# Head-wise loads of eight tokens per partition, turned by column tiles, in an attention + MLP kernel

## The chip, the cores and the metric

The kernel runs on one core of one Trainium2 chip. The metric is the device time of one execution in microseconds (us). Executions of one kernel agree within about 0.3%, and all timed comparisons below use runs of the fast state; two kernels had a single look, whose state is unknown, and of them only durations of single instructions are read. "Start" below means the first matmul that multiplies by `w_in`, "end" the end of the last matmul, both read from the trace of the profiled run; "dense part" is the time between, "tail" the time from the end to the end of the span. Each set of rounds ran on one chip, with the kernel before run along (medians of 206.90 to 207.19 us).

One thing bears on every reading of the first 14 us: TensorE's clock. The records of the granted clock begin only when it first rises to full; the profile prints 1.00 ahead of that, but there the clock is half. In the kernel before, plain matmuls of 128 columns start 107 ns apart until 9.3 us and 56 ns apart from 10.4 us on, and the first record is at 10.33.

## The reference, cut to what matters

```python
# q, k, v: (4, 8, 768, 64) fp32, drawn * 0.1; w_in (512, 2048), w_out (2048, 512); n_global 8, n_local 96
scores = q @ k.T / 8 + bias(-slope[h] * distance)      # masked to a local window of 96 and 8 global keys
a = softmax(scores)
x = (a @ v)  -> (3072, 512)
h = x @ w_in
out = (h - tanh(h)) @ w_out
```

Because q and k are drawn with a factor of 0.1, the distance bias dominates the scores. The comparison with the reference therefore hardly notices q and k in a wrong order.

## The kernel before

The work is cut into 24 tiles of 128 queries with all 8 heads. A tile is loaded (q, k, v), its q and k are turned so that the head dimension lies on partitions, scores are multiplied, exponentiated and masked, multiplied with v, scaled, and turned again to become the moving operand of the first product (`w_in`). Pairs of tiles then take the second product (`w_out`), for some groups as a Strassen product of seven. The program does not state an order: a planner in it simulates all engines with assumed durations and writes each engine's instructions in the order that comes out. Each engine then works through its own instructions in that order.

The loads: 256-byte rows, one token of one head each, that is 8 rows per partition. The three first (k of tile 0, q of tiles 0 and 1) are hardware loads in fp32 that VectorE casts to bf16; all others are issued by GpSimd and are cast on the way.

```python
hw_loads = {("k", 0): SP, ("q", 0): SP, ("q", 1): ACT}
...
def rows(src, u):
    b, i = tiles[u]
    return src[b, :, i * P : (i + 1) * P, :].rearrange("h p d -> p h d")
```

The turn: four plain transposes of 128 columns into one PSUM bank, in bf16, then one copy out.

```python
def pe_T(bank, src):
    t = bank.bitcast(BF16)
    for p in range(NP):                                  # NP = 4 pairs of heads
        nc.tensor.transpose(t[:, p * P : (p + 1) * P], src[:, p * P : (p + 1) * P], ident)
...
pl.op(("T", nm, u), PE, 0.24, lambda ...: pe_T(...))
pl.op(("Te", nm, u), [(DVE, 0.345), (ACT, 0.48)], None, lambda ...: copy(...))
```

Masking and the product with v work on all eight heads at once; the second product is in Strassen form for the groups in FAST; the last group's last two products share one bank:

```python
FAST = set(range(5, 14))
...
pl.op(("M", u, o), DVE, 0.61, lambda ...: a_M(u, o), after=[E half 0, E half 1, mask half 0, mask half 1])
...
HOME = {3: ("in", 0), 4: ("in", 1), 1: ("one", 0), 5: ("mid", 0), 2: ("mid", 1), 7: ("out", 0), 6: ("out", 1)}
...
if g == LAST:
    for t, kk in enumerate((7, 6)):
        pl.op(("cs", g, t), DVE, 0.335, ...)             # sum of the bank and what was kept
        pl.op(("st", us[t], 1), SP, 0.6, ...)            # store of 128 KB
```

The softmax here doesn't subtract the row's maximum and nothing guards it: scores larger than these inputs give would overflow.

## Time and profile before

| | before |
|---|---|
| time, median of 3 runs | 207.09 us (206.95 to 207.3) |
| span of the profiled run | 205.1 us |
| start / end / tail | 16.16 / 201.38 / 3.76 us |
| first tile's q landed, its first scores | 6.83, 9.61 us |
| first two parts of `w_in` landed | 14.8, 18.2 us |

The prediction shows the lines. In a row of the timeline the columns are start, length, engine, line of the program, operation, written tile, read tiles, shapes and count, and in brackets how long the engine had been idle and what ended that. Landing times are of the DMA records in the trace. One line is added here because the change replaces it: the turn of k tiles before, as durations of the single matmuls (least, median and most in ns). Matmuls overlap, so the pace is seen from start to start: it is 56 ns at the full clock.

```profile
L461 PE MATMUL bank<-ident,kb x28: 219/219/314, 6.5 to 41.0; 128*128 128x128 bf16 x28
```

### The profile page before, as it was taken

The numbers are of one execution on the slowest core, as the hardware profiler recorded it, in microseconds if no ns is written. First come the engines' busy times: TensorE is split into PE (matmuls) and PEld (weight loads), VectorE is DVE, ScalarE is ACT, GpSimd is POOL, SyncE is SP. The second block draws the span as 40 slices with busy tenths as digits, with TensorE's granted clock in tenths as the row PEclk, the third lists the DMA queues.
The fourth block names the chain that finished last, engine by engine and source line by source line (L and its number), as shares of the span: only waits on it lengthen the run. The fifth ranks groups of instructions, "written<-read, shape, count | busy, mean of one in ns | idle before, by whom it ended". The sixth has DMA issues, their size and how long they took to land.

```text
span 205.1 us, 5929 instructions
## 1 busy us (share of the span) xinstructions
PE 197.7 (96%) x2339; PEld 167.3 (82%) x2339; DVE 176.4 (86%) x387; ACT 139.7 (68%) x326; POOL 68.1 (33%) x83
## 2 busy tenths in 40 slices
PE   7789999999999999999999999999999999999992
PEld 5568997579867779889898898898898898888881
DVE  5698899989886888899999879979979979699683
ACT  6699878275787886996987777667677665434310
POOL 8985363680552250542251351351350000000000
PEclk9999999999999999999999999999999999999999
DMA  6999999999999999999999999998998504002023
GB/s 141 158 184 199 186 204 192 170 186 151 178 196 203 135 101 162 82 139 194 124 89 226 106 101 109 189 114 111 184 116 90 151 6 128 3 0 102 3 102 102
DMA packets 110971, 27.28 MB, mean 133 GB/s; under 512 B 103008, under 2 KB 108128, under 8 KB 110944
## 3 DMA queue, kind: packets, MB, share of 16 engines
q0 software_dynamic: 76512, 13.24, 88.5%
q1 hardware_dynamic: 32864, 13.38, 34.2%
q10 hardware_dynamic: 1568, 0.30, 0.8%
q8 instruction: 18, 0.29, 0.6%
q14 instruction: 9, 0.07, 0.1%
HBM read 27.30 MB, written 6.29 MB: 164 GB/s over the span
## 4 chain that ended last, share of the span: by engine, by line
PE 88%; DMA 7%; DVE 2%; ACT 1%; issue 0%; DVEq 0%
PE bank L476 39%; PE bank L347 28%; PE bank L517 7%; PE bank L412 5%; DMA qT<-qb 5%; PE bank L431 3%; PE bank L433 2%; DMA ot<-in_q_dram 2%; PE bank L461 2%; PE bank L714 1%; DVE pd L422 1%; ACT x L448 0%; DVE kT L402 0%; DVE qb L402 0%; ACT pd L417 0%
## 5 line engine op out<-in xcount | busy, mean ns | idle before, releaser
L476 PE MATMUL bank<-xT,w_in_bf 128*128 128x256 bf16 (+1 forms) x896 | 95.2, 257 | 0.2 <-ACT pd L417 0.2
L476 PEld LDWEIGHTS <-w_in_bf 128*128 128x128 bf16 x896 | 75.6, 98 | 8.7 <-issue 0.3
L803 ACT ACTIVATE th<-bank 128x512 f32<-128x512 f32 x96 | 56.8, 610 | 32.0 <-PE bank L476 28.8
L485 DVE TENSOR_TENSOR g<-bank,th 128x512 bf16<-128x512 f32 x80 | 53.0, 683 | 8.2 <-ACT th L803 7.9
L626 POOL DMA_DIRECT2D kb<-in_k_dram x23 | 20.3, 884 | 72.9 <-PE bank L476 68.6
L347 PEld LDWEIGHTS <-hb 128*128 128x128 bf16 x416 | 40.1, 98 | 5.2
L347 PE MATMUL bank<-bsum,hb 128*128 128x256 bf16 x256 | 32.9, 273 | 0.0
L417 ACT ACTIVATE pd<-bank 128x512 bf16<-128x512 f32 x48 | 26.1, 601 | 6.4 <-PE bank L412 6.4
L321 DVE TENSOR_TENSOR hb<-g 128x1024 bf16<-128x1024 bf16 x45 | 29.6, 683 | 0.2
L417 ACT ACTIVATE po<-bank 128x512 bf16<-128x512 f32 x40 | 22.3, 623 | 0.0
L626 POOL DMA_DIRECT2D vb<-in_v_dram x24 | 21.6, 899 | 1.8 <-DMA w_out_bf<-in_moe_w_out_dram 1.6
L448 ACT ACTIVATE x<-bank,rden 128x64 bf16<-128x64 f32 x84 | 19.4, 316 | 3.6 <-DVE rden L440 3.2
L422 DVE TENSOR_TENSOR pd<-pd,mk 128x1024 bf16<-128x1024 bf16 x24 | 16.5, 688 | 5.6 <-ACT pd L417 5.5
L626 POOL DMA_DIRECT2D qb<-in_q_dram x22 | 19.9, 904 | 3.7 <-DMA w_out_bf<-in_moe_w_out_dram 3.5
L347 PE MATMUL bank<-w_out_bf,hb 128*128 128x256 bf16 x160 | 20.6, 273 | 0.0
L347 PE MATMUL bank<-bsum,g 128*128 128x256 bf16 x144 | 18.4, 273 | 0.0
L321 DVE TENSOR_TENSOR ot<-bank,sum 128x512 f32<-128x512 f32 (+1 forms) x21 | 13.8, 661 | 2.2 <-PE bank L347 1.8
L347 PEld LDWEIGHTS <-g 128*128 128x128 bf16 x144 | 13.8, 98 | 1.8
L412 PE MATMUL bank<-qT,kT 64*128 64x128 bf16 x352 | 14.5, 219 | 0.4 <-DMA qT<-qb 0.2
L422 DVE TENSOR_TENSOR po<-po,mk 128x1024 bf16<-128x1024 bf16 x20 | 13.7, 685 | 1.2 <-ACT po L417 1.1
L412 PEld LDWEIGHTS <-kT 64*128 64x128 bf16 x352 | 10.3, 95 | 5.1 <-issue 4.3
L431 PE MATMUL bank<-vb,pd 128*128 128x65 bf16 x192 | 14.1, 193 | 0.1
(57 smaller groups left out, 184.2 us busy)
## 6 DMA issues: line engine op xcount, KB each, us to landing
out_dram<-ot SPq DMA_DIRECT2D x9, 512.0 KB, 3.4
vb<-in_v_dram POOLq DMA_DIRECT2D x24, 128.0 KB, 5.7
kb<-in_k_dram POOLq DMA_DIRECT2D x23, 128.0 KB, 5.0
qb<-in_q_dram POOLq DMA_DIRECT2D x22, 128.0 KB, 5.4
w_out_bf<-in_moe_w_out_dram POOLq DMA_DIRECT2D x4, 512.0 KB, 13.3
w_in_bf<-in_moe_w_in_dram POOLq DMA_DIRECT2D x3, 512.0 KB, 10.8
out_dram<-ot SPq DMA_DIRECT2D x5, 256.0 KB, 4.5
w_in_bf<-in_moe_w_in_dram POOLq DMA_DIRECT2D x2, 256.0 KB, 8.9
```

Of the source, the lines that this page charges most:

```text
L321: eng_of(e).tensor_tensor(out=out, in0=x, in1=y, op=ALU.add if sign > 0 else ALU.subtract)
L347: nc.tensor.matmul(o, a, b, start=(f == 0), stop=(f == CH - 1))
L412: nc.tensor.matmul(t[hh][:, p * P : (p + 1) * P], kt[r, p, :], qt[r, p, :], start=True, stop=True)
L417: nc.scalar.activation(dst, t, AF.Exp, bias=0.0, scale=scale)
L422: nc.vector.tensor_tensor(out=p, in0=p, in1=mk[:, m, :, :], op=ALU.mult)
L431: nc.tensor.matmul(o, pd[:, slot(h), :], vd[:, h, 0 : Dh + 1], start=True, stop=w is None)
L448: nc.scalar.activation(x[:, h, :], t[:, h, 0:Dh], AF.Copy, bias=0.0, scale=rd[:, h, :])
L476: nc.tensor.matmul(t[:, (f - fa) * n : (f - fa + 1) * n], w_in_bf[j][:, c, fo : fo + P], xt[:, c, 0:n], start=(c == 0), stop=(c == CD - 1),)
L485: nc.vector.tensor_tensor(out=dst, in0=t.rearrange("q (b n) -> q b n", n=n), in1=th.rearrange("q (b n) -> q b n", n=n), op=ALU.subtract,)
L517: nc.tensor.matmul(o, gblk(g, f, f + 1, t * P, t * P + P)[:, 0, :], w_out_blk(f, 0, DM), start=(f == 0), stop=(f == CF - 1),)
L626: pl.op(key, POOL, 0.88, lambda e, u=u, src=src, dst=dst: nc.gpsimd.dma_start(out=dst(), in_=rows(src, u)), after=[prev and ("issue", prev ...
L803: pl.op(("th", g, f), ACT, 0.48, lambda e, g=g, f=f: nc.scalar.activation(buf("th", ("th", g, f)), buf("bank", ("h", g, f)), AF.Tanh, bias ...
```

## The change

Its intent: q and k of the first four tiles are loaded with 2 KB rows. A partition then holds 8 tokens of one head (16 partitions for each of 8 heads) instead of one token of all heads, so the usual transpose does not fit. Eight pairs of matmuls do the turn instead: for token j of the eight, the stationary operand is the 64 columns of that token, the moving operand a slice of the identity that picks the even or the odd heads, and the two heads of a pair are written to the two halves of the partitions by two column tiles of TensorE. Around it: masks, products with v and scaling by head parity for the first six tiles; group 4 in Strassen form; three banks and three stores at the last group; a new order of tiles and of loads.

```diff
-    TILES = [(1, 0), (0, 0), (0, 1), (1, 1), (0, 2), (3, 0), (0, 3), (3, 1), (2, 0), (2, 1), ...]
+    TILES = [(1, 0), (0, 0), (0, 1), (1, 1), (0, 2), (3, 0), (3, 1), (3, 2), (1, 2), (2, 0), ...]
-    FAST = set(range(5, 14))
-    NPE = 7
-    NPX = 8
+    FAST = set(range(4, 14))
+    N8 = 4
+    HSPLIT = 6
+    NPE = 8
+    NPX = 6
...
+    TJ = 8
+    def rows8(src, u):
+        b, i = tiles[u]
+        return src[b, :, i * P : (i + 1) * P, :].rearrange("h (t j) d -> t h (j d)", j=TJ)
...
+    def pe_T8(bank, src):
+        o = bank.rearrange("e (p t j) -> e p t j", p=NP, j=TJ)
+        i8 = ident.rearrange("k (t p s) -> k s p t", p=NP, s=2)
+        for j in range(TJ):
+            for s in range(2):
+                nc.tensor.matmul(
+                    o[s * Dh : (s + 1) * Dh, :, :, j], src[:, j * Dh : (j + 1) * Dh], i8[:, s], start=True, stop=True,
+                )
...
-                pl.op(("T", nm, u), PE, 0.24,
-                      lambda e, u=u, nm=nm: pe_T(buf("bank", ("T", nm, u)), buf(nm + "b", (nm + "b", u))),
+                pl.op(("T", nm, u), PE, 0.55 if u < N8 else 0.24,
+                      lambda e, u=u, nm=nm: (pe_T8 if u < N8 else pe_T)(buf("bank", ("T", nm, u)), buf(nm + "b", (nm + "b", u))),
...
+            if u < HSPLIT:
+                for hh in range(2):
+                    pl.op(("M", u, o) if hh else ("Mp", u, o), DVE, 0.335, lambda e, u=u, o=o, hh=hh: a_M(u, o, hh, hh + 1),
+                          after=[("E", u, o, hh), masks[hh], ("issue", ("Mp", u, o)) if hh else None])
...
-            for t, kk in enumerate((7, 6)):
+            for t, c0, c1, key, tag in ((0, 0, DH, ("P", g, 7), "out2"), (1, 0, DH // 2, ("Pp", g, 6), "out"),
+                                        (1, DH // 2, DH, ("P", g, 6), "out3")):
```

## The prediction

> **What bounds the kernel now.** I read, in this order: the busy shares and the slices of the page, the chain of waits that ended last, the timeline of the first 25 us, the table of stretches over the same part, and the timeline of the last 10 us.
>
> From the page:
>
> ```profile
> PE 197.7 (96%) x2339; PEld 167.3 (82%) x2339; DVE 176.4 (86%) x387; ACT 139.7 (68%) x326; POOL 68.1 (33%) x83
> PE   7789999999999999999999999999999999999992
> DMA  6999999999999999999999999998998504002023
> PE 88%; DMA 7%; DVE 2%; ACT 1%; issue 0%; DVEq 0%
> ```
>
> TensorE is on the chain for 88% of the span, and only the first three slices and the last are not full. (A busy TensorE can still be slow, so I count paces below.) The DMA engines are full from the second slice to beyond the middle. The candidates for a gain are therefore the first 16 us, TensorE's amount of work, and the last 4 us.
>
> The chain in order of time gives the paces of undisturbed stretches:
>
> ```profile
> 0.74 4.60 DMA ot<-in_q_dram
> 14.09 0.96 ACT x L448 x4
> 16.16 1.05 PE bank L476 x16
> 17.70 1.79 PE bank L476 x32
> 36.70 3.45 PE bank L517 x16
> 40.16 0.87 PE bank L347 x8
> 193.52 7.87 PE bank L347 x72
> ```
>
> The first product runs at 56 ns for each 128-column matmul (1.79/32), the direct second product at 216 ns for 512 columns (3.45/16), a Strassen product at 109 ns for 256 columns (0.87/8). Priced so, the work after 16.16 us is: first product 640 x 0.109 + 256 x 0.056 = 84.2; Strassen 560 x 0.109 = 61.2; direct 64 x 0.216 = 13.8; scores, some 290 at 35 ns, 10.2; probabilities times v, 330 at 30 ns, 10.1; transposes 48 x 0.056 = 2.7. Sum 182.2 us, while 16.16 to the last matmul's end at 201.4 is 185.2. The missing 3 us is about what some 36 changes between the score form and the full form cost at 0.1 us (a block of eight after one takes 0.98 instead of 0.87). So from 16.16 us there is practically no stall. The start of the dense part sets the end.
>
> The timeline before it:
>
> ```profile
> 6.51 0.61 PE L461 MATMUL bank<-ident,kb 128*128 128x128 bf16 x4 [1.43 <-DVE kb L402]
> 7.50 0.57 DVE L402 CAST qb<-ot 128x512 bf16<-128x512 f32 x1
> 9.61 0.61 PE L412 MATMUL bank<-qT,kT 64*128 64x128 bf16 x8
> 10.25 1.09 ACT L417 ACTIVATE pd<-bank 128x512 bf16<-128x512 f32 x2 [2.02 <-PE bank L412]
> 11.77 0.68 DVE L422 TENSOR_TENSOR pd<-pd,mk 128x1024 bf16<-128x1024 bf16 x1
> 15.11 0.88 POOL L626 DMA_DIRECT2D kb<-in_k_dram  x1 [0.89 <-DMA w_in_bf<-in_moe_w_in_dram]
> 15.59 0.42 DVE L402 COPY xT<-bank 128x512 bf16<-128x512 bf16 x1
> 18.51 0.74 POOL L598 DMA_DIRECT2D w_out_bf<-in_moe_w_out_dram  x1 [1.77 <-DMA w_in_bf<-in_moe_w_in_dram]
> ```
>
> Two strands meet at 16.16: the first tile's attention (its q, cast at 7.50, to its transposed output, done at 16.01), and the first part of w_in. GpSimd's waits say when weights landed: its 16th issue is released by w_in at about 15.1, the 18th at 18.4. I take these for the first and second part of w_in (the 8th and 10th issues); the second is about when the rest of the first tile's product can begin. The strand of loads has no more than 1 us of slack.
>
> **What the Trainium skill says.** "DMA: Bandwidth & Descriptors", section "Why small descriptors are slow (HBM only)", puts about three cycles of overhead on a packet: 11 instead of 8 cycles for 256 bytes. The trace agrees in size. GB/s in the next rows counts bytes as landed, in bf16, half of what these loads read:
>
> ```profile
> 8.00:10.00 2.00, 2.00 (x22) 1.64 (x20) 1.20 (x4) 0.23 (x2) 2.00 (x3) 1.00 2.42 154
> 12.00:14.00 2.00, 1.84 (x37) 1.41 (x32) 2.00 (x7) 2.00 (x5) 2.00 (x3) 1.00 1.25 205
> ```
>
> With 256-byte rows in flight it is 154 GB/s, so 128 KB take 0.85 us; with 2 KB rows of the weights 205 GB/s, so 0.64 us. "TensorEngine Tiling (Array Packing)", sections "Key Properties" and "Restrictions": tiles can run in parallel, a change of tiling drains the engine, and column tiling excludes fast weight load. The trace shows the drain (the 0.98 above); this kernel has no column tile, so the rest is not shown. "PSUM — Partial Sum Buffer", section "PSUM bank collisions raise a hardware error", says two engines must not touch a bank at once; that is why, in the tail, both last additions wait for the very last matmul.
>
> **The change part by part.**
>
> (1) Loads. All eight q and k loads of the first four tiles come before the first part of w_in, before and after, so each saves 0.85 - 0.64 = 0.21 us of a full DMA: 8 x 0.21 = 1.7 us. Three are hardware loads in fp32, for which I have no clean rate, so I take 1.5 us. The first w_in part then lands at about 13.6 and the second at 16.9. The first tile's hardware loads, which took 3.9 and 5.6 us to land, should take 3 to 4: its q is castable at about 5 to 5.5 instead of 7.
>
> (2) Turning. A tile was turned by four matmuls (4 x 0.056 = 0.22 us); now by 16 with 64 columns each. With 30 ns, the pace of the 65-column matmuls here, they take 0.5 us, with the lost fast weight load up to 0.9. Eight turns cost 2 to 5 us more, in a stretch where TensorE multiplies zeros or waits: of 16.16 us only about 4.8 are useful. Little of it should reach the end. The PSUM copy out is now fp32: about 0.6 instead of 0.42 us, 8 x 0.2 = 1.6 us of VectorE and ScalarE, of which 0.4 lies on the first tile's strand.
>
> (3) Halves by head parity for six tiles. For the first tile, mask (0.68 in one piece), product, reciprocal and scaling can start with the first exponential; I count 0.5 us off the strand from 9.61 to 16.01. With (1) it is ready near 13.6 to 14.2. The strand gains 1.8 to 2.4, the loads 1.5 at the second weights part. I take the dense start 1.9 us earlier, all told.
>
> (4) Group 4 goes to Strassen: 32 x 0.216 = 6.9 against 56 x 0.109 = 6.1 us: 0.8 us less. It costs VectorE about 5.5 us (five sums of 0.68, evictions) in a region where it has 10 to 25% free, and ScalarE is relieved by 1.2.
>
> (5) Transposes elsewhere: one more tile's q and k on TensorE, two tiles' outputs fewer: eight matmuls each way, zero.
>
> (6) The tail. Now:
>
> ```profile
> 199.47 1.91 PE L347 MATMUL bank<-bsum,hb 128*128 128x256 bf16 x16
> 201.42 0.76 DVE L321 TENSOR_TENSOR ot<-bank,sum 128x256 f32<-128x256 f32 x2 [0.33 <-PE bank L347]
> 201.87 0.82 SPq L547 DMA_DIRECT2D out_dram<-ot  x2
> ```
>
> Both additions (0.76) follow the last matmul and two issues (0.82) follow the first. With three banks, only one addition of 128 columns (estimate 0.3, from 0.42 for 256) and one issue of 0.41 remain behind it: the last issue ends near 202.2 instead of 202.7. Gain 0.5 us.
>
> (7) New order of tiles and of issues, one more buffer each for kb, qb and x: with no stall to remove, zero, give or take 0.5.
>
> Sum: 1.9 + 0.8 + 0.5 = 3.2 us. I give back 0.2 for turns that fall into the dense part and their extra drains. 207.1 - 3.0 = 204.1; the tuning hints that the start was fitted to the new loads, so I round to **204.0 us**.
>
> **Rivals.** (a) Vector and Scalar bind the head: VectorE is busy all of 12 to 16 us and ScalarE all of 12 to 16, and each first-phase tile needs from VectorE more (four subtractions, two masks, scaling, copies: about 6 us) than TensorE's 3.6 us of first product. Then the earlier loads buy under 1 us: 205.5. For it: these rows; against it: ScalarE idles 2 us ahead of 10.25 and VectorE several short times before it. (b) The turn is slow: at 0.9 us or more, eight turns (7 us) plus 3 us of other useful work overfill the 9 us before the start; the head gains nothing: 205.8. For it: no fast weight load; against it: the pairs may overlap. (c) Loads alone bind the start: the attention is ready first, and TensorE fills the time to the second w_in part with the first quarter of four tiles (4 x 0.89 us): 2.8 us in the head, 203.1 or less. For it: the 1 us between 15.1 and 16.16; against it: (a). (d) Strassen's sums at group 4 make VectorE the bound from 40 to 70 us, eating the 0.8: 204.8.
>
> **Range and chances.** (a), (b) and (d) pull up by 0.8 to 1.8, (c) down by 1; they exclude each other in part. Range 202.5 to 205.7. Faster by over 2% means under 202.95, which asks for (c) and a little more: 0.23. Slower by 2% (211.2) would need a new stall that lasts through the dense part: 0.01. Within 2%: 0.76.
>
> **What would show it.** The first w_in matmul at 13.5 to 14.8 us instead of 16.16; GpSimd's waits for w_in ending 1.5 us earlier; the fp32 loads landing within 4 us; a turn's 16 matmuls within 0.5 to 0.6 us; 616 + 8 Strassen and 32 direct matmuls; no TensorE idle between the start and the last 4 us; last matmul to end of the span 3.2 instead of 3.7 us. I am wrong if the dense start moves by less than 1 or more than 2.8 us, if TensorE has gaps between 16 and 70 us, or if a turn takes near 1 us.

## The result, and the profile after

The changed kernel took **209.44 us** in the median (209.32 to 209.52, 4 runs), the kernel before 207.19 us in the same rounds (206.95 to 207.44, 4 runs). A ratio here and below is the mean time of one kernel's runs over the mean of the other's of the same rounds, so it is not quite the ratio of the medians: 1.0108, 95% interval 1.0091 to 1.0126. Executions over 1.5% slower than the fastest of the same kernel are left out of the means. By the measure of 2% that is "same", but it is 1% slower, on the wrong side of zero and well outside the range of 202.5 to 205.7.

| | before | after | difference | predicted |
|---|---|---|---|---|
| start | 16.16 | 18.54 | +2.38 | -1.9 |
| dense part | 185.22 | 184.67 | -0.55 | -0.6 (Strassen -0.8, +0.2 back) |
| tail | 3.76 | 4.47 | +0.71 | -0.5 |
| span | 205.14 | 207.68 | +2.54 | -3.0 |

So the middle did what was predicted and both ends went the other way. The page of the kernel after, against the lines of before in the prediction:

```profile
PE 200.5 (97%) x2464; PEld 173.0 (83%) x2464; DVE 183.4 (88%) x403; ACT 140.7 (68%) x332; POOL 66.3 (32%) x83
PE   6899999999999999999999999999999999999991
PE 89%; DVE 5%; DMA 2%; issue 1%; ACT 0%; DVEq 0%; ACTq 0%
```

TensorE is busier than before, 200.5 instead of 197.7 us, which is no gain: it is busy with the turns. The third digit of its row, which was 8 before, is now full. The chain of waits in order of time (start, length, what) shows where:

```profile
5.96 5.02 PE bank L477 x80
10.98 0.55 PE bank L425 x16
11.53 1.05 PE bank L477 x16
...
14.09 1.03 PE bank L477 x16
...
15.47 1.03 PE bank L477 x16
...
18.61 1.00 PE bank L499 x16
```

L477 is the new turn. It is on the chain eight times: five turns back to back take 5.02 us, the three others 1.03 to 1.05 us each, 8.1 us in all. The timeline over the same stretch tells how the first tile gets behind:

```profile
10.91 0.62 PE L425 MATMUL bank<-qT,kT 64*128 64x128 bf16 x16
11.34 2.06 ACT L430 ACTIVATE pd<-bank 128x512 bf16<-128x512 f32 x4 [3.99 <-PE bank L425]
12.60 0.69 DVE L415 CAST qT<-bank 128x512 bf16<-128x512 f32 x1 [0.89 <-PE bank L477]
13.21 0.75 DVE L435 TENSOR_TENSOR pd<-pd,mk 128x512 bf16<-128x512 bf16 x2
14.02 1.10 PE L477 MATMUL bank<-ident,kb 128*64 128x64 bf16 x16
15.40 1.10 PE L477 MATMUL bank<-ident,kb 128*64 128x64 bf16 x16
16.41 0.88 POOL L656 DMA_DIRECT2D qb<-in_q_dram  x1 [2.64 <-DVE x L464]
18.54 1.07 PE L499 MATMUL bank<-xT,w_in_bf 128*128 128x128 bf16 x16
```

The first scores start at 10.91 instead of 9.61, since five turns stand ahead of them in TensorE's order. The first mask starts at 13.21 instead of 11.77: VectorE takes its work in order too, and ahead of the mask stands the copy out of a later turn, for which it waited 0.89 us while the first exponentials were done. From mask to start it is 5.33 us instead of 4.39, with two more turns in between. So 1.44 us of the delay of 2.38 arose before the mask and 0.94 after it. GpSimd, which also waits in order, was held for 2.64 us at 16.41 by this strand; with two more loads standing ahead of it in the new order, the first part of `w_out` was issued at 19.1 instead of 16.0 and landed at 31.2 instead of 29.3.

How long a turn is inside: 1.10 us less the 0.30 us that a single one of these matmuls lasts, over the seven steps from pair to pair, is 0.115 us per pair. In the records the two matmuls of a pair start 2 to 8 ns apart. They do run side by side; it is the pair that is slow, 115 ns for 64 columns where 65 columns of another product take 30 ns. The clock is not the reason: the turns ahead of 10.2 us, where it rose to full, have the pace of those behind it.

The tail of the kernel after, timeline of the last 5 us:

```profile
203.35 0.82 DVE L324 TENSOR_TENSOR ot<-bank,sum 128x256 f32<-128x256 f32 x3 [0.46 <-PE bank L354]
203.80 1.59 SPq L570 DMA_DIRECT2D out_dram<-ot  x3
```

One store issue more stands in line (1.59 us for three instead of 0.82 for two); 0.30 us of that is the second of the three, which took 0.68 us. And the first of the three sums, whose product was done 0.88 us before the end of TensorE, does not start until 0.14 us after that end.

### The profile page after: what moved, and what is told of

Same layout as the page of the kernel before. It is cut to its first block, busy times and chain, and to the rows that moved or that the text cites. A ratio compares the mean times of both kernels' runs of the same rounds, so it can differ in the third digit from the quotient of the medians.

```text
span 207.7 us, 6184 instructions
## 1 busy us (share of the span) xinstructions
PE 200.5 (97%) x2464; PEld 173.0 (83%) x2464; DVE 183.4 (88%) x403; ACT 140.7 (68%) x332; POOL 66.3 (32%) x83
## 4 chain that ended last, share of the span: by engine, by line
PE 89%; DVE 5%; DMA 2%; issue 1%; ACT 0%; DVEq 0%; ACTq 0%
PE bank L499 41%; PE bank L354 28%; PE bank L425 5%; PE bank L477 4%; PE bank L540 3%; PE bank L445 3%; PE bank L447 2%; DMA ot<-in_k_dram 2%; PE bank L484 2%; DVE ot L324 1%; DVE hb L324 1%; DVE pd L435 1%; DVE g L508 1%; DVE po L435 1%; DVE qT L415 0%
## 5 line engine op out<-in xcount | busy, mean ns | idle before, releaser
L354 PEld LDWEIGHTS <-hb 128*128 128x128 bf16 x464 | 44.1, 98 | 5.7
L656 POOL DMA_DIRECT2D kb<-in_k_dram x20 | 17.7, 884 | 74.0 <-PE bank L499 63.4
L354 PE MATMUL bank<-bsum,hb 128*128 128x256 bf16 (+1 forms) x288 | 35.4, 270 | 0.0
L324 DVE TENSOR_TENSOR hb<-g 128x1024 bf16<-128x1024 bf16 x50 | 32.6, 684 | 0.2
L656 POOL DMA_DIRECT2D qb<-in_q_dram x20 | 17.8, 888 | 9.3 <-PE bank L499 5.5
L354 PE MATMUL bank<-bsum,g 128*128 128x256 bf16 x160 | 20.4, 273 | 0.0
L435 DVE TENSOR_TENSOR pd<-pd,mk 128x1024 bf16<-128x1024 bf16 (+1 forms) x30 | 17.1, 578 | 3.1 <-ACT pd L430 3.1
L324 DVE TENSOR_TENSOR ot<-bank,sum 128x512 f32<-128x512 f32 (+2 forms) x24 | 15.2, 641 | 3.6 <-PE bank L354 3.5
L354 PEld LDWEIGHTS <-g 128*128 128x128 bf16 x160 | 15.5, 98 | 2.0
L435 DVE TENSOR_TENSOR po<-po,mk 128x1024 bf16<-128x1024 bf16 (+1 forms) x23 | 14.1, 618 | 1.5 <-ACT po L430 1.3
L413 ACT COPY vb<-vb 8x512 bf16<-8x512 bf16 x14 | 8.6, 614 | 9.9 <-PE bank L447 9.9
## 6 DMA issues: line engine op xcount, KB each, us to landing
w_out_bf<-in_moe_w_out_dram POOLq DMA_DIRECT2D x4, 512.0 KB, 10.3
```

The source lines that it names most:

```text
L324: eng_of(e).tensor_tensor(out=out, in0=x, in1=y, op=ALU.add if sign > 0 else ALU.subtract)
L354: nc.tensor.matmul(o, a, b[:, c0:c1], start=(f == 0), stop=(f == CH - 1))
L413: nc.scalar.copy(out=dst, in_=src)
L435: nc.vector.tensor_tensor(out=p, in0=p, in1=mk[:, m, s0 * NP : s1 * NP, :], op=ALU.mult)
L656: else nc.gpsimd.dma_start(out=dst(), in_=rows(src, u)),
```

## The experiments

Where an expectation speaks of T, that is the theory that the turn is slow and lies on the way to the start; the rivals are named in the texts: the loads, the tail, the order of the plan. Every kernel is a change of the kernel after, unless the text says that it is of the kernel before. In e1, e2, h1, v5 and the f kernels the durations that the planner assumes are those of the kernel after (h1 and v5 add one small copy to the plan); in the others it plans anew, and the order can shift with the edit.

### Is it the turn? A plain one in its place

```diff
-        (pe_T8: 16 matmuls)
+        for p in range(NP):
+            nc.tensor.matmul(bank[:, p * P : (p + 1) * P], src[:, p * P : (p + 1) * P], ident, start=True, stop=True)
```

This is the kernel after with four plain matmuls of 128 columns; q and k of four tiles are wrong.

> The changed kernel with its 16 small matmuls of a turn replaced by four ordinary ones of 128 columns (a wrong result on purpose; same loads, same order of instructions, same fp32 copy out). Theory T (the turn holds TensorE in front of the first tile: 8 x 1.03 us instead of 8 x 0.22, so some 6 us of it on the way): the first w_in matmul comes at 15 us or earlier instead of 18.5, the time falls from 209.4 to 206.4 or less. Rival L (loads no sooner, DMA engines out of step): start at 17.5 or later, 208.5 or more. Rival O (the new order of tiles and issues makes the head late): the same as L.

Measured: 207.82 us, ratio to before 1.0048 (1.0033 to 1.0063); start 16.84, dense part 184.63, tail 4.57. The start comes 1.7 us earlier than after's and the time falls by 1.6, so most of the loss at the head is the turn. Two of its turns, one at the half and one at the full clock, and the start:

```profile
10.98 0.61 PE L474 MATMUL bank<-ident,qb 128*128 128x128 bf16 x4
12.95 0.39 PE L474 MATMUL bank<-ident,kb 128*128 128x128 bf16 x4
16.84 1.07 PE L494 MATMUL bank<-xT,w_in_bf 128*128 128x128 bf16 x16
```

But the start is still later than before's 16.16, though this kernel has the larger rows and the halves by parity: with a turn as cheap as the old one, the head has gained nothing. The first tile's q landed at 7.54 us, and the clock was half until 12.4 us. The result lies between what the turn as the only cause asked for (206.4 or less) and what the rivals did (208.5 or more): the turn is the larger part and not the whole.

### Why does a pair take 115 ns?

The candidates are the loading of 64-column weights, the moving operand, whose columns are 16 bytes apart (every eighth element of the identity), and the writes, 32 bytes apart in PSUM. Three kernels, all wrong, take them one at a time:

```diff
 f2: stationary operand of 128 columns, so no column tile; moving operand and writes strided as before
+            c = min(j, TJ - 2) * Dh
+            nc.tensor.matmul(o[:, :, :, j], src[:, c : c + 2 * Dh], i8[:, s], start=True, stop=True)
 f4: as f2, but the moving operand contiguous
+            nc.tensor.matmul(o[:, :, :, j], src[:, c : c + 2 * Dh], ident[:, 0:Dh], start=True, stop=True)
 f5: as f2, but the writes contiguous
+            nc.tensor.matmul(bank[:, j * Dh : (j + 1) * Dh], src[:, c : c + 2 * Dh], i8[:, s], start=True, stop=True)
```

> The changed kernel with the same 16 matmuls of 64 moving columns in a turn, but with 128 columns stationary instead of 64 (full array, a wrong result on purpose). If the 64 ns of each are the slow loading of a 64-column weight tile, the pace falls to about 30 ns, a turn to 0.5 us, and the time to about 207.5. If it is the number of matmuls or the 32-byte strides of their writes: 64 ns and 209.3 as before.

> One look. As the wide turn (16 matmuls, 128 columns stationary, 64 moving, wrong result on purpose), but the moving operand is contiguous and only the writes to PSUM keep their 32-byte stride. The pair of small matmuls took 117 ns in the changed kernel, a wide one 115 ns. If the strided writes cost it: still about 115 ns a matmul, a turn of 1.9 us. If the strided reads of the moving operand cost it: about 30 ns, a turn of 0.5 to 0.6 us.

> One look. The counterpart: contiguous writes, moving operand with its 16-byte stride, 128 columns stationary (wrong result on purpose). If the strided reads cost it: about 115 ns a matmul; if the writes: about 30 ns. If both this and the run with strided writes are near 30 ns or both near 115, neither stride alone is the cause and slow weight loading is left.

One turn of sixteen in the chain of waits of each, first f2, then f4, then f5:

```profile
19.41 1.85 PE bank L478 x16
```

```profile
13.84 0.89 PE bank L478 x16
```

```profile
20.51 1.83 PE bank L478 x16
```

f2: 116 ns per matmul, now one after another, so the kernel got slower still: 216.32 us, ratio 1.0459, start 25.33. Weights of 128 columns do not help; the loading of 64-column weights was not the limit. f5, with the writes put right, keeps 114 ns. f4, with the moving operand put right, needs 56 ns (208.81 and 219.68 us for f4 and f5, single looks of unknown state, so only the durations count). The clocks differ, half for all of f5's turns and full for all of f4's, but f2 settles it: its pace is 116 ns both ahead of 9.5 us, where its clock rose, and behind. At the full clock, then, it is 116 ns with both strides (f2) and 56 ns with the strided writes alone (f4). The moving operand's step of 16 bytes is the cost, and the strided write is a smaller one, about twice the 30 ns of a contiguous product. This says also that a pair of column tiles costs as much as one such matmul: the tiling worked.

The Trainium skill has this, in a place where I did not look: "SBUF — State Buffer", section "Door 1: The DMA port swizzle", notes that SBUF is read in lines of 16 bytes, that full bandwidth needs at least two accesses to a line, and that PSUM has lines of 8 bytes, so that non-contiguous access slows matmuls. The steps here, 16 and 32 bytes, reach a new line with every element. The trace agrees, with 114 and 56 ns against some 30.

### A turn that is right and contiguous

The moving operand is a permuted copy of the identity, made once; the writes are contiguous; the copy out of PSUM does the permutation.

```diff
+    ident8 = cpool.tile([P, 2, Dh], BF16, name="ident8")   # even and odd heads, packed
 ...
-                    o[s * Dh : (s + 1) * Dh, :, :, j], src[:, j * Dh : (j + 1) * Dh], i8[:, s], start=True, stop=True,
+                    bank[s * Dh : (s + 1) * Dh, j * Dh : (j + 1) * Dh], src[:, j * Dh : (j + 1) * Dh], ident8[:, s, :],
+                    start=True, stop=True,
 ...
-     copy(e, dst, bank)
+     copy(e, dst.rearrange("d p (t j) -> d p t j", j=TJ), bank.rearrange("d (j p t) -> d p t j", j=TJ, p=NP))
```

> The changed kernel, right result, with the same 16 column-tile matmuls of a turn, but contiguous on both sides: a permuted identity stored contiguously as moving operand, contiguous writes, and the order put right by the copy out of PSUM. If strides cost the 117 ns of a pair: 30 to 60 ns a pair, a turn of 0.3 to 0.6 us, start near 16.5, 206.9 to 207.5. If it is the loading of 64-column weights[...]: still about 109 ns, a turn of 0.9 to 1.0 us, 209.

Two turns in the timeline of h1:

```profile
10.84 0.64 PE L476 MATMUL bank<-ident,qb 128*64 128x64 bf16 x16
...
14.37 0.44 PE L476 MATMUL bank<-ident,kb 128*64 128x64 bf16 x16
```

and one stretch of its table of stretches, in which the number after the busy times is the granted TensorE clock:

```profile
10.00:12.00 2.00, 2.00 (x33) 1.40 (x30) 1.33 (x3) 1.68 (x4) 2.00 (x4) 0.50 1.23 204
```

At the full clock a turn takes 0.44 us from first start to last end: 0.244 without the last matmul's own 0.196, or 35 ns per pair. At the half clock, granted from 7.2 to 14.0 us in this run, it is 0.64 us. TensorE had been busy for only 0.30 of the 2 us from 4 to 6 and 0.78 of the next 2. The Trainium skill, "TensorE: Matmul & The Clock Gate", section "What's actually happening", gives half the clock as the state at first and again after an idle window of some 3.4 us. The trace agrees with the half, 0.50, but the stretch before the fall was not idle: from 3.8 to 7.2 us TensorE was busy for 1.2 us.

The time is 207.28 us (207.11 to 207.4), ratio 1.002 (1.0005 to 1.0035), 2.16 us less than after. By the traces, 1.35 of the 2.35 us in the span are the start (17.19), 0.34 the dense part (184.33), and 0.66 the tail (3.81), to which the turn contributes nothing; more on that below. The start is still 1 us later than before's. All four runs of h1 show the low mean clock of 0.982 to 0.983, so the long half clock belongs to this kernel's time; what it may be worth is told with v5 below.

A middle way was to give a partition 4 tokens of a pair of heads, 1 KB rows, with 8 matmuls of 128 moving columns (right):

```diff
-        return src[b, :, i * P : (i + 1) * P, :].rearrange("h (t j) d -> t h (j d)", j=TJ)
+        return src[b, :, i * P : (i + 1) * P, :].rearrange("(p s) (t j) d -> t p s (j d)", s=2, j=TJ)   # TJ = 4
 ...
+                nc.tensor.matmul(o[s * Dh : (s + 1) * Dh, :, :, j], src[:, c : c + Dh], ident, start=True, stop=True)
```

> The changed kernel with 4 tokens of a head pair per partition (1 KB rows) and a turn of 8 matmuls (64 columns stationary, 128 moving) instead of 16 of 64 by 64; right result. If the 64 ns of a small matmul are the loading of its 64 weight columns, a turn takes 8 x 64 = 0.5 us and the time falls by about 2 us to 207.4 (theory T). If the pace grows to 128 ns (moving columns or the strided writes set it), a turn stays at 1.0 us and the time at 209.4. Rivals L and O: 209.4 whatever the turn takes.

Measured: 206.87 us, ratio 0.9997 (0.9982 to 1.0012), start 16.04, dense part 184.69. Pairs follow each other by 109 ns, but there are four of them instead of eight. It is level with before.

### Are the loads worth anything?

e3 is the kernel after with the old rows and the old turn everywhere (`N8 = 0`).

> The changed kernel with the loads and turns of the kernel before (256-byte rows, four transposes), all else kept. T: the head is as before or better (start 15.5 to 16.5), the dense part 0.6 us shorter, the tail 0.8 longer: 206.5 to 207.5. L: the same. O: start still near 18 us, 208.5 to 209.5.

Measured: 206.78 us, ratio 0.9994 (0.9978 to 1.0011); start 16.52, dense part 184.83, tail 3.82. Without the new rows and the new turn most of what they cost at the head is gone (16.52 against 18.54, before 16.16); what is left of the change is level with before.

The three first loads are hardware loads. v5 is h1 with the old rows and the old turn for these three alone:

```diff
-    ... if u < N8 else ...
+    ... if u < N8 and (nm, u) not in hw_loads else ...      # rows, turn and copies, five places
```

> The changed kernel with the contiguous turn, but the three hardware loads (first tile's k and q, second tile's q) with their old 256-byte rows and four transposes. If 2 KB rows brought these three nothing: the first tile's q still lands at 6.8 to 7.3 and the time is 206.8 to 207.3, as with them or less. If they are worth the 0.2 us each that I counted: q lands 0.5 us later and 207.8.

Measured: **206.15 us** (205.96 to 206.5), ratio 0.9954 (0.9931 to 0.9977): faster than the kernel before by half a per cent, which is below the measure of 2% but clear of the noise. Start 16.19, dense part 184.38, tail 3.80. Its start, in the timeline:

```profile
16.19 1.07 PE L499 MATMUL bank<-xT,w_in_bf 128*128 128x128 bf16 x16
```

The first tile's q landed at 7.35 us here with 256-byte rows, at 7.07 (after) and 7.23 (h1) with 2 KB rows, at 6.83 in the kernel before and 6.60 in e3. So the row length did not bring it forward. What 2 KB rows did change is the issue of these loads: 0.69 and 0.82 us in the trace of after, 0.46 and 0.59 before, so that the second load on the same queue starts later. They also changed which of the first two comes first: with them the second tile's q landed at 4.4 instead of 5.3 us, and the first tile's k, which is needed sooner, at 5.5 instead of 4.7. Of the 1.0 us by which v5 starts ahead of h1, a part can be the clock, which is half for 3.4 us less in v5. It looks small: w1, below, has the loads and turns of v5 and half the clock until 13.1 us, 1.7 us longer than v5, and starts 0.17 us later.

Does an earlier q at least give an earlier end? g0 is the kernel before with the first tile's q and the second's swapped on the two hardware queues:

```diff
-hw_loads = {("k", 0): SP, ("q", 0): SP, ("q", 1): ACT}
+hw_loads = {("k", 0): SP, ("q", 0): ACT, ("q", 1): SP}
```

> The kernel before with one edit: the first tile's q is loaded by ScalarE's queue as the first DMA, and the second tile's q takes its place as the second of SyncE's queue. If the landing of the first tile's q (6.8 us in every run so far, 2 KB rows or not) holds the strand to the first product, it lands at about 5.3, and the start moves from 16.2 to 15.0 to 15.5, where the first part of w_in binds: 206.0 to 206.5. If it doesn't hold it: 207.0.

Measured: 208.08 us, ratio 1.0057 (1.0039 to 1.0074), slower. The q landed at 5.64 instead of 6.83, the first scores came at 7.74 instead of 9.61, the start at 15.55 instead of 16.16. But the dense part took 186.32 us instead of 185.22. TensorE's waits in it from 15.5 us on (engine, tile, line, what it waited for: total, times, longest):

```profile
PE bank L476 <- DVE xT L402: 0.7, 1, 0.7
PE bank L461 <- DMA kb<-in_k_dram: 0.4, 1, 0.4
```

The second tile was not ready when the first one's product was done: its q, which gave up the first place, landed at 7.00 instead of 5.3 us. So the start was moved at the price of the second tile, and that was worth nothing.

### The tail

e4 is the kernel after with the old tail: one bank, two stores.

> The changed kernel with the last sums and stores of the kernel before (one bank, two stores). If the third store and the late first addition cost what the traces say (4.5 instead of 3.7 us from the last matmul to the end), the time falls by 0.8 us to 208.6. If the longer tail is only shifted measurement of the end: no change, 209.4.

Measured: 209.24 us, ratio 1.0123 (1.0104 to 1.0141), tail 4.21 instead of 4.47. The expected gain was missed; it is 0.2 us, within the scatter. The DMA records show another thing in the tail of both e4 and after, on a queue of its own:

```profile
q14 instruction: 1, 0.01, 0.4%
```

(queue and kind, packets, MB and share of the engines in the last 8 us of after). It is one block of 8 KB of instructions. Its place divides the kernels:

| fetch, seen from TensorE's end | kernels: tail in us |
|---|---|
| 0.8 to 1.1 us after it | after 4.47, e1 4.57, e2 4.31, f2 4.48, f4 4.51, f5 4.43 (three banks, three stores); e4 4.21 (one bank, two stores); v3 3.90 (two banks, two stores) |
| 1.3 to 1.7 us ahead of it | e3 3.82, h1 3.81, v5 3.80 (three banks, three stores); v1 3.81 (one bank, two stores); v2 3.56, g2 3.56, w1 3.58, w2 3.55 (two banks, two stores) |
| none in the tail | before 3.76, e5 3.74, h3 3.73, g0 3.74 (one bank, two stores) |

With the late fetch every tail is longer by 0.3 us or more than the same tail without it. The lines of e3, whose TensorE ends at 201.35, against those of after above:

```profile
201.14 0.82 DVE L324 TENSOR_TENSOR ot<-bank,sum 128x256 f32<-128x256 f32 x3
201.59 1.31 SPq L570 DMA_DIRECT2D out_dram<-ot  x3
```

In after the first sum starts 0.14 us after TensorE's end, in e3 0.21 us before it; and the second store's issue takes 0.68 us in after, 0.38 in e3. These 0.35 and 0.30 us are the 0.65 by which the two tails differ (4.47 and 3.82), of the 0.71 us that the tail lost against before. The sum is late before the record of the fetch begins, at 1.05 us, so by the records the transfer itself did not hold it; what did is open. In v3 the sum is in time, and there the first store takes 2.2 us from issue to landing instead of 1.7. Apart from the fetch, the three banks with three stores are worth nothing against the old tail (3.80 to 3.82 against 3.73 to 3.81), and two banks with two stores are worth 0.2 us. The Trainium skill, "Runtime: NRT & Kernel Launch", section "Instruction fetch mechanics", says that crossing the boundary of a block, 16 KiB there, is mostly hidden; that fits the early place here and not the late one. This is a sorting of traces: I could move the fetch only with the rest of the program, and no run changed it alone.

Another sign that the loads did not set the start: in e4 the first two parts of `w_in` landed at 14.8 and 16.8 us, in after at 15.8 and 18.0; the two programs differ in the last group alone. Both start at the same time, 18.59 and 18.54.

### The parts in the kernel before

e5 puts only the new rows and the slow turn into the kernel before; h3 does so with the contiguous turn; v1 only puts group 4 into Strassen form; v2 is v1 with two banks in the tail.

```diff
 e5: + rows8, pe_T8 and the fp32 copy for u < 4, planner's durations as before
 h3: e5, with the contiguous turn of h1
 v1: -FAST = set(range(5, 14))
     +FAST = set(range(4, 14))
 v2: v1, and in the last group
     +return {7: ("out2", 0), 6: ("out", 0)}.get(kk, HOME[kk]) if g == LAST else HOME[kk]
```

> The kernel before with only the 2 KB rows and the 16-matmul turn for its first four tiles; its own order of tiles, issues and tail. Theory T (the turn's 64 ns a matmul) : eight turns of 1.03 us, all in front of the first w_in matmul, delay it from 16.2 to about 18 to 19, time 209 to 210, as much as the whole change. Rival O (the new order is what costs): 207 to 207.5. If the loads gained what I predicted and the turn were free: 205.5.

Measured: 211.7 us, ratio 1.0224 (1.0198 to 1.0251), start 20.87, dense part 185.97. In before's order the slow turn costs even more than in after's.

> The kernel before with only the 2 KB rows and this contiguous turn. With the strided turn the same kernel took 211.7. If strides cost it: 207 to 208 (turns no longer hold TensorE; the first tile's q still lands near 7). If the weights cost it: about 211.

Measured: 207.92 us, ratio 1.0044 (1.0028 to 1.0061), start 16.98, dense part 186.25. The turn's pace alone is worth 3.8 us in this order; the larger rows still give no earlier start.

> The kernel before with one edit: group 4 by Strassen too. If the step of my prediction was right (32 x 0.216 against 56 x 0.109 us of a full TensorE): 0.8 us less, 206.1. If VectorE, with some 5.5 us more to do between 30 and 60 us, takes it back: 206.9.

Measured: 208.48 us, ratio 1.0063 (1.0038 to 1.0089), start 16.09, dense part 186.89: 1.7 us longer than before, with less work. TensorE's waits from 16 us on in v1:

```profile
PE bank L433 <- DVE po L422: 0.8, 2, 0.5
PE bank L431 <- DVE pd L422: 0.4, 1, 0.4
```

In the kernel before, the longest wait over the same stretch is 0.2 us. TensorE now waits for masks, at 59, 61 and 81 us: VectorE, with five more sums, is late, as the prediction's rival (d) said. All its waits together are 1.7 us, against 0.4 in the kernel before, and the order has four more changes between the score form and the full form (44 against 40), 0.4 us at the prediction's 0.1 us each. The loss is 1.7 us plus the 0.8 us of work saved, so about 0.8 us stay unexplained. In the kernels with the new order of tiles the dense part is 184.3 to 185.0 us, with the exception of f5 (185.6) and v3, told below. So group 4 in Strassen form loses in the old order. That it pays in the new one is inferred from the dense part, 0.55 us below before's: no run has the new order without it.

> The same with the last two products in a bank each and the two old stores: the first sum and store can go before the last matmul's end. If that takes one issue (0.45 us) out of the tail: 205.7; if the stores' landing sets the end anyway: 206.1.

Measured: 208.07 us, ratio 1.0049 (1.0024 to 1.0074), 0.4 us less than v1, tail 3.56 instead of 3.81. Two banks and two stores gain what three banks and three stores were meant to gain.

Another theory was that the plan itself was bad: the planner assumed 0.55 us for a turn and 0.345 us for the copy. v3 is h1 with the two-bank tail, with measured durations in the planner, and with one mended dependency. (In the kernel after, a mask by head parity waits for one half of the mask's building, while each parity has heads in both halves. The order that came out happened to be right.)

```diff
-                pl.op(("T", nm, u), PE, 0.55 if u < N8 else 0.24,
+                pl.op(("T", nm, u), PE, 0.42 if u < N8 else 0.24,
-                pl.op(("Te", nm, u), [(DVE, 0.345), (ACT, 0.48)],
+                pl.op(("Te", nm, u), [(DVE, 0.62), (ACT, 0.55)] if u < N8 else [(DVE, 0.345), (ACT, 0.48)],
```

> The changed kernel with the contiguous turn, two banks and two stores in the tail, and the order planned with measured durations (a turn 0.42, a copy out 0.62 us); right result. If the wrong plan held the first tile: start at 15.5 to 16, 205.0 to 205.8. If not, start near 17 as in the contiguous run, 206.8 or so (0.4 us for the tail alone).

Measured: 210.94 us, ratio 1.0185 (1.0159 to 1.0211). The start is early, 16.3, some 0.9 us ahead of h1's as the theory asked for, but the dense part takes 188.67 us. TensorE's waits from 20 to 40 us:

```profile
PE bank L448 <- DVE po L436: 1.0, 1, 1.0
PE bank L499 <- ACT x L463: 0.6, 1, 0.6
```

They make 1.6 of the 4.3 us by which the dense part exceeds h1's; the rest was not traced. Here truer durations gave a better start and a worse order behind it, so the theory of the wrong plan does not explain the loss as a whole; a wrong duration in the planner can be part of an order that works.

### What is best

g2 is e2 with the first q first (the swap of g0) and a tail of two banks and two stores:

> The changed kernel with 1 KB rows of head pairs and a turn of 8 matmuls, the first tile's q loaded first, and a tail of two banks and two stores (the first of which can now go before the last matmul's end). Theory: 206.9 of the pair rows, less 0.4 for the tail (no third issue of 0.45 us) and less about 1 for the earlier q: 205.4 to 205.9. If q's landing is not what holds the start: 206.5.

Measured: 205.35, 206.0, 207.51 and 207.19 us, ratio 0.9982 (0.9937 to 1.0028). The profiled run started at 15.06 and had the shortest span of all, 203.57 us, but the runs of this kernel lie 2 us apart, so nothing follows.

w1 is v5 with two banks and two stores and the mended mask; w2 is the same with every load as before (`N8 = 0`).

```diff
-            halves = [0, 1] if g == LAST and kk == 6 else [1]
+            halves = [1]
-            ... (1, 0, DH // 2, ("Pp", g, 6), "out"), (1, DH // 2, DH, ("P", g, 6), "out3")):
+            ... (1, 0, DH, ("P", g, 6), "out")):
```

> The changed kernel with the contiguous turn for the five GpSimd loads, the old 256-byte rows for the three first hardware loads, and the last group's products 7 and 6 in two banks with two stores. If the gains add: v5 (206.15, tail about 4.4 us) less 0.4 us of tail, that is 205.6 to 205.9, ratio near 0.993, first w_in matmul at 16.0 to 16.5 us, tail 3.5 to 3.8 us. If the tail's gain is eaten elsewhere (another order of the whole plan, an instruction fetch that falls into the tail): 206.1 or more.

Measured: **206.0 us** (205.89 to 206.16, 6 runs), ratio 0.9953 (0.9939 to 0.9968); start 16.36, dense part 184.35, tail 3.58. The tail gained 0.2 us over v5 and the start lost as much, so it is level with v5 and lies between the two expectations, 0.1 us above the range for gains that add. The tail in its timeline:

```profile
200.52 0.76 DVE L325 TENSOR_TENSOR ot<-bank,sum 128x256 f32<-128x256 f32 x2
200.98 0.82 SPq L570 DMA_DIRECT2D out_dram<-ot  x2
```

No wait stands ahead of the sums; in the kernel before it was 0.33 us.

> The same kernel, but every load with the old 256-byte rows and the old turn (what is left of the change: new tile order, masks and products by head parity, group 4 in Strassen form, two-bank tail). If the 2 KB rows of the five GpSimd loads (0.6 instead of 0.83 us each, some 1 us of the queue) are worth anything at the end, it is slower than w1 by 0.5 to 1.0 us: 206.2 to 206.8. If the rows of 2 KB bring nothing that lasts, both are within 0.3 us of each other.

Measured: 206.61 us (206.14 to 206.74), ratio 0.998 (0.9965 to 0.9994); start 16.37, dense part 185.04, tail 3.55. Against w1 the larger rows of the five GpSimd loads are worth 0.6 us. They do not act on the start, which is the same, but behind it, in the dense part (184.35 against 185.04). How is not shown: the second part of `w_in` landed at 16.7 instead of 18.9 us, but in e3, with the old rows too, it landed at 17.1, with a dense part of 184.83; and the planner ordered w1 and w2 by different durations.

## Why the prediction was wrong, point by point

**The step that failed** is step (2): "With 30 ns, the pace of the 65-column matmuls here, they take 0.5 us, with the lost fast weight load up to 0.9", and "Little of it should reach the end". A turn took 1.03 us, not 0.5, for the step of 16 bytes in its moving operand (116 ns per matmul in f2, 56 in f4) and not for the weights (f2); eight turns are 8.1 us, where the step had 4 to 7. And a part of it reached the start, since turns of later tiles stand ahead of the first tile's work in the order of TensorE, and their copies ahead of its masks in the order of VectorE. I had counted the time in which TensorE multiplies zeros as free for the turns. It is free in sum, but a turn in the queue is ahead of something. The cheap turns show the size: 1.35 us of start with h1, 1.7 with e1, of the 2.38 that were lost. The rest goes with the new rows of the hardware loads, as far as v5 shows it, or in a small part with the clock. The step also priced the old turn at the full clock, 0.22 us; ahead of 10.3 us its four matmuls took 107 ns each (the 1.00 in the prediction's row for 8 to 10 us stands for a missing record). Rival (b) had the slow turn, at 205.8, but let the head gain nothing, where it lost 2.4 us.

**Step (1), the loads,** was right in size for GpSimd's loads: 0.59 to 0.66 us from landing to landing with 2 KB rows (after, w1), 0.83 to 0.89 before, as predicted from 205 and 154 GB/s. Its landing times for `w_in`, 13.6 and 16.9, came true in some traces and not in others, whatever the turn: 13.7 and 16.9 in e5, 13.8 and 15.9 in f2, 13.9 and 16.5 in v5, but 15.8 and 18.0 in after and 15.2 and 16.7 in w1. What scatters them is open. For the three hardware loads the step was wrong: "its q is castable at about 5 to 5.5", and it landed at 7.07. Ahead of it nothing was gained by rows (v5), and the larger rows cost issue time and fp32 copies of 0.69 us instead of 0.42.

**Step (3), halves by parity, 0.5 us:** not to be seen. From the first q's landing to the start it is 9.33 us before, and 9.92 in e3 and 9.63 in w2, which have the halves with the old turn; v5 has 8.84, w1 9.32. The clock does not hide it: before, e3, w2 and v5 have 3.4 or 3.5 us of half clock in that stretch, w1 has 6.0.

**Step (4), Strassen for group 4, -0.8 us:** right in sum (-0.55 net in the dense part, -0.6 predicted), but not by itself: without the new order it turns into a loss of 1.7 us (v1). So **step (7)**, the order at zero, was probably wrong as a term: the order seems to be what lets step (4) pay, though no run has the order alone.

**Step (6), the tail, -0.5 us:** wrong. It lost 0.7, of which 0.65 go with an instruction fetch that I had not thought of: 0.35 us of a late first sum and 0.30 of a long second issue. Without that, three banks and three stores come out level with the old tail: the third issue in line takes back what the shorter sum gives. Two stores and two banks are worth 0.2 us.

**The frame,** "the start of the dense part sets the end", holds when the stretch behind the start stays the same. It held for after, e1, h1 and v5; g0 and v3 show where it does not: an earlier start bought with a late second tile or late masks comes back as waits of TensorE.

**Step (5)** was not tested. Open are about 0.8 us of v1, how much of each start is the clock's, whether the fetch causes the longer tail or only goes with it, and why the first tile's q lands between 6.6 and 7.5 us in kernels that differ little.

## What to carry to other kernels

Price a small matmul by how its operands lie, not by its columns alone: here a permuted identity copied once into packed form and a contiguous write made the same turn 35 instead of 115 ns per pair at the full clock (53 to 57 ns at the half). An engine that works in order has no free time ahead of the critical strand: ask of every added instruction what stands behind it. And test a bundle by its parts, because one part of this one lost 1.7 us when it stood alone (Strassen without the order), one cost more than all gained (the strided turn), and rows of 2 KB were worth 0.6 us only for the loads that form the queue's stream. Last, check the clock by the pace of a plain matmul: in all 20 traces here, plain matmuls ahead of the first clock record ran at half the clock, under a printed 1.00.

## What the Trainium skill lacked or had wrong

- "SBUF — State Buffer", section "Door 1: The DMA port swizzle", has the 16-byte and 8-byte lines, but among the DMA ports; other pages repeat them, and none gives a figure for what they cost a matmul. The runs show, for 64 columns in bf16: 114 to 116 ns with a moving operand stepped by 16 bytes (f2, f5), 56 ns with writes stepped by 32 bytes (f4), 35 ns per pair of column tiles with both contiguous at the full clock (h1).
- "TensorE: Matmul & The Clock Gate", section "Back-to-back issue gap", has a table of the gap by the number of columns alone, with some 25 ns for 1 to 64 columns. With strided operands it was 114 to 116 ns (f2, f5); a pointer to the lines of SBUF would belong there.
- "TensorEngine Tiling (Array Packing)", section "Restrictions", says that column tiling shuts off the fast weight load, but not what that costs. Here little of it is to be seen: with contiguous operands a pair, weights included, took 35 ns at the full clock.
- "Runtime: NRT & Kernel Launch", section "Instruction fetch mechanics", calls the crossing of a block mostly hidden. In eight traces a block of 8 KB was fetched about 1 us behind the last matmul, and their tails, 3.9 to 4.6 us, were 0.3 us or more above the same tails with an earlier fetch or none, 3.55 to 3.82 us (sorted, not tested).
- "DMA: Bandwidth & Descriptors", section "Why small descriptors are slow (HBM only)": right for GpSimd's loads (0.59 to 0.66 instead of 0.83 to 0.89 us), but no page says that first hardware loads may gain nothing from larger rows: the first tile's q landed at 7.07 with 2 KB (after) and 6.83 with 256 bytes (before), and the issue itself grew from 0.46 and 0.59 to 0.69 and 0.82 us.
